# An S4D convolution and a gMLP block on one core: a planner that also hands out the cosines', parameters' and kernel products' places in PSUM, spectra of even and odd chunks kept apart, and a last chunk transformed in two halves

## The chip, the core and the metric

The kernel runs on one core of a Trainium2 chip. The core has a matrix engine (TensorE, PE in the profile; its weight loads are listed as PEld), a vector engine (VectorE, DVE), an activation engine (ScalarE, ACT), GpSimd (POOL) and SyncE (SP), which here only issues transfers. Each engine works through its own queue in order. All five meet through semaphores. The operands lie in SBUF; the matrix engine writes to PSUM, which has room for eight places of 128 x 512 float32 words. The metric is the device time of one execution in microseconds (us); lower is better.

## The reference, cut to what matters

```python
h  = x + ssm(layernorm(x))                 # x: 1 x 2048 x 512
h2 = h + gmlp(layernorm(h))

def ssm(u):                                # S4D: one long convolution for each of 512 channels
    dt = exp(log_dt);  A = -exp(log_A_real) + 1j*A_imag;  C = (C_real + 1j*C_imag)*dt
    K = 2*einsum("dn,dnl->dl", C, exp(A*dt*l)).real        # 128 terms, 2048 positions
    return irfft(rfft(u, 4096) * rfft(K, 4096))[:2048] + u*D_skip

def gmlp(x):
    z = gelu(x @ w_in);  z1, z2 = halves(z)
    g = w_sp @ layernorm(z2) + b_sp
    return (z1 * g) @ w_out
```

Everything is float32, and the large products of the gMLP are made from three float32r products each (high x high, high x low, low x high).

## The kernel before, in words

The first phase (`phase_a`) makes the convolution. The 512 channels are four **chunks** of 128. The kernel K of a chunk comes from eight **units**, 16 channels each, so there are 32 units. A unit (function `unit`) does this: TensorE makes the phases of 2 x 512 exponentials (tile `ph`, two PSUM places); ACT and DVE take off whole turns (ACT into `cs`, which is a part of `wb`; DVE into `f`); ACT takes sines into `ph` and cosines into `ce` (a PSUM place) and back into `cs` (SBUF); POOL makes three tables of magnitudes (`m`, a part of `wa`) from the chunk's tables `mt`; DVE multiplies the sines and cosines by them; TensorE forms the kernel piece with 32-wide products, back into the first half of `ph`; ACT copies it to one of six buffers `ks`. `ph` exists twice, and the second unit waits for the first one's copy to `ks` before it can write there again.

The two transforms are products too, cut into pieces. Per chunk there are eight of each: **a** (first step of the input's transform, 8 matmuls), **b** (second step, 4 matmuls; its result is the spectrum `ka`), **c** (first step for the kernel, from `ks`), **d** (second step for the kernel, 4 matmuls, whose PSUM result DVE multiplies into `ka` and `kb`), and **e** (back transform from `ka` and `kb`, 8 matmuls). Between b and d two transfers write `kb`, which is `ka` with its halves of partitions exchanged. The pieces a, b, c and e are copied out of PSUM by ACT. All pieces and all small steps take their PSUM places from three tiles `fft`. There is one pair `ka`, `kb`, so b of a chunk waits for e of the chunk before.

Ahead of the first unit stand the parameters of chunk 0 (`params`: some twenty DVE and ten ACT instructions on 128 x 128, then eight transfers to DRAM, `scr_stk`, from where POOL's queue loads `sw`, the left operand of a unit's first product), the tables `mt`, and the layer norm of the input (`norm_x`, 64 statistics on DVE, then 64 scalings that ACT, DVE and POOL share by the fixed string `NORM`). The parameters of chunk 1, and those of 2 and 3 together, come between the first units.

The order of all that is set by a planner (class `Plan`). Each call on an engine is recorded with a duration and its dependences, `list_schedule` lays them out forwards and backwards by rules of engine, PSUM place and shared SBUF port, `schedule` repeats it with random shifts and keeps the shortest plan, and the calls are then issued in the plan's order. Since `issue` makes all these calls, nearly all of phase A's instructions have one line in the profile, L424. They are told apart by tile.

Next come `phase_b1` (last step of the back transform, tile `y`, L882; layer norm; first half of the gMLP's input product, L916), `phase_b2` (second half, L965) and `phase_b3` (mixing over positions, L1051; output product, L1034). They are ordered by the framework, not by `Plan`. The transfers that `phase_b1` needs (`xq`, `g`, `w1r`) are issued by SP as soon as phase A's buffers under them are free, and the split of `w1r` (L808, L809) stands inside phase A's last pieces: it is issued behind the copy that `last` names.

Of the kernel before, what the change touches and what calls it, by code (L numbers as in the profile page):

```python
# [12 lines left out]
I32 = mybir.dt.int32  # L13
# [13 lines left out]
NORM = "aavaapav"  # L27
# [4 lines left out]
TRIES = 60  # L32
# [145 lines left out]
class Plan:  # L178
# [4 lines left out]
    HOP = 0.2  # L183

    def __init__(self, nc, banks):
        self.nc, self.banks, self.ops, self.live, self.t, self.step = nc, banks, [], {}, 0.0, 0.0
        self.nbank, self.open = 0, None
        for e in self.ENGINES:
            setattr(self, e, _Engine(self, e))
# [4 lines left out]
    def bank(self, shape):  # L194

        self.nbank += 1
        n = math.prod(shape[1:])
        names = "abc"[:len(shape) - 1]
# [4 lines left out]
    @contextmanager  # L203
    def group(self, dur):

        self.open = dict(calls=[], aps=[], eng=None, dur=dur)
        yield
        g, self.open = self.open, None
        self._add(**g)

    def _resolve(self, x, bank=None):
        return x.view(self.banks[0] if bank is None else bank) if isinstance(x, Late) else x

    def call(self, e, method, args, kw, dur=None):
# [10 lines left out]
        return self._add(calls, aps, e, dur)  # L225

    def _add(self, calls, aps, eng, dur):
        e, method, args, kw = calls[0]
        o = dict(id=len(self.ops), eng=self.ENGINES[eng], calls=calls, t=self.t, deps={}, banks=set(), func=None, lat=0.0)
        self.t += self.step  # L230
        o["port"] = False
        views = [(self._resolve(x), w) for x, w in aps]
        spaces = [str(v.space) for v, _ in views]
        out, ins = views[0][0], [v for v, w in views[1:] if math.prod(v.shape[1:]) > 1]
        n = math.prod(out.shape[1:])
        isps = ["PSUM" in str(v.space) for v in ins]
        if o["eng"] == "DVE":
            ins = ins or [out]
            two = method not in ("tensor_scalar", "tensor_scalar_add", "tensor_scalar_mul", "tensor_copy", "memset", "bn_stats",
                                 "reciprocal")  # L240
            c = math.prod(ins[0].shape[1:]) if method == "bn_stats" else n
            ps = any(isps) or "PSUM" in str(out.space)
            if two or ps or method == "bn_stats":
                d = 0.15 + c / 960
            elif method == "reciprocal":
                d = 0.15 + c / 160
            else:
                d = 0.15 + c / 1920
            o["port"] = not ps and method not in ("bn_stats", "reciprocal", "memset")
        elif o["eng"] == "ACT":  # L250
            d = 0.18 + n * 0.00083
            f = str(args[2]).split(".")[-1] if method == "activation" else "Copy"
            o["func"] = {"Exp": "exp", "Sin": "sin", "Arctan": "sin"}.get(f)
        elif o["eng"] == "POOL":
            d, o["port"] = 0.3 + n * 0.0022, True
        elif o["eng"] == "PE":
            d = 0.4
        else:
            d = 0.06
        if method == "dma_start":  # L260
            nb = 4 * out.shape[0] * n if out.shape else 0
            o["lat"] = 2.0
            o["dma"] = nb / 250e3
            o["port"] = False
            if o["eng"] == "POOL":
                d = 0.7
        o["dur"] = dur if dur is not None else d
        for (x, w), (v, _) in zip(aps, views):
            key = x.key if isinstance(x, Late) else v.tensor.name
            if isinstance(x, Late):  # L270
                o["banks"].add(x.key)
            if isinstance(key, str) and key.startswith("in_"):
                continue
            self._touch(o, key, v, w)
        o["names"] = {v.tensor.name for v, _ in views}
        self.ops.append(o)
        return o
# [27 lines left out]
    def prepare(self):  # L305
# [8 lines left out]
        for ids in holders.values():  # L314
            for i in ids[1:]:
# [9 lines left out]
    def list_schedule(self, want, back=False):  # L325
# [9 lines left out]
        ready, free = {e: [] for e in engines}, {e: 0.0 for e in engines}  # L335
        est, start, end = [0.0] * n, [0.0] * n, [0.0] * n
        banks, held, until, uses = [(0.0, i) for i in range(len(self.banks))], {}, {}, dict(self.uses)
        port = dma = last = 0.0
        table = None
        for i in range(n):  # L340
            if not left[i]:
                ready[ops[i]["eng"]].append(i)
        for _ in range(n):
            best = None
            for e in engines:
                cand = []
                for i in ready[e]:
                    t = max(est[i], free[e])
                    if i in self.bank_of and self.bank_of[i] not in held:
                        if not banks:  # L350
                            continue
                        t = max(t, min(banks)[0])
                    if ops[i]["port"]:
                        t = max(t, port)
                    cand.append((t, i))
                if cand:
                    soon = min(cand)[0] + 0.25
                    w, i, t = min((want[i], i, t) for t, i in cand if t <= soon)
                    if best is None or (t, w, i) < best:
                        best = (t, w, i)  # L360
            t, _, i = best
            o = ops[i]
            e = o["eng"]
            ready[e].remove(i)
            b = self.bank_of.get(i)
            if b is not None and b not in held:
                x = min(banks)
# [801 lines left out]
```

## Time and profile before

Three runs took 988.8, 991.05 and 990.53 us (median 990.53). The profiled execution took 990.94 us.

| | us |
|---|---|
| profiled execution | 990.94 |
| its span, first to last instruction | 989.2 |
| PE busy in the span | 866.9 |
| DVE busy | 546.4 |
| ACT busy | 397.2 |
| POOL busy | 230.1 |
| first y matmul (end of phase A) | 393.95 |

Times below are counted from the span's start. A row of a grouped view gives line, engine, operation, "out<-in", shapes, count, then the busy time in us and the mean duration of one in ns, then the engine's idle time just before these instructions and what ended it. "fft", "ka", "wb" and so on are tiles; `x` is the tile x1 (the input's first step, and before that the parameters of chunk 0), `a` is a2 (a constant). One matmul of these float32 products is two rows in counts from the trace and one in the listings of the order.

### The profile page before, as it was taken

To read this page: it belongs to the slowest core of one execution; us is meant where nothing else is said; L and a number is where in the kernel's file an instruction comes from. 1 tells how busy PE (TensorE), PEld (TensorE's weight loads), DVE (VectorE), ACT (ScalarE), POOL (GpSimd) and SP (SyncE) were. 2 spreads that over 40 slices of the span, in tenths; PEclk is the share of its full clock that TensorE was granted. 3 is DMA by queue.
4 is the path that set the end of the run, shared out by engine and by line. 5 is a ranking of instruction groups with operands and counts; after the bars stand their busy time and mean duration, and the time that the engine had idled before them with its cause. 6 is when DMAs were issued, how large, how long until landed. Compare 5 with 4: busy or idle time off the path is not lost.

```text
span 989.2 us, 16700 instructions
## 1 busy us (share of the span) xinstructions
PE 866.9 (88%) x6936; PEld 735.0 (74%) x6936; DVE 546.4 (55%) x994; ACT 397.2 (40%) x657; POOL 230.1 (23%) x185
## 2 busy tenths in 40 slices
PE   0245798988989978889999999999999999999994
PEld 0134687867978868878889998888888888888883
DVE  6989979998669743955427783135113311431142
ACT  4287868758766723153434442122012201211110
POOL 3656575668764600000001110000000000000010
PEclk9999999989999978989999999999999999999997
DMA  9102220061040194645341113124223422332221
GB/s 343 32 17 99 63 55 2 12 143 34 10 108 12 34 338 174 181 129 138 119 159 43 32 32 107 54 66 126 65 63 96 129 59 80 88 105 64 64 64 53
DMA packets 45386, 88.84 MB, mean 90 GB/s; under 512 B 4480, under 2 KB 19712, under 8 KB 42880
## 3 DMA queue, kind: packets, MB, share of 16 engines
q1 hardware_dynamic: 43872, 85.17, 28.7%
q0 software_dynamic: 1440, 2.62, 1.0%
q8 instruction: 54, 0.88, 0.4%
q14 instruction: 20, 0.16, 0.1%
HBM read 59.99 MB, written 19.40 MB: 80 GB/s over the span
## 4 chain that ended last, share of the span: by engine, by line
PE 77%; DVE 15%; ACT 3%; issue 3%; DMA 1%; SPq 0%; DVEq 0%; ACTq 0%
PE g L1051 31%; PE fft L424 14%; PE pz L916 8%; PE pz L965 8%; PE po L1034 6%; PE ph L424 5%; DVE f L424 3%; DVE ka L424 3%; PE y L882 3%; DVE wb L424 2%; DVE big L424 2%; PE pl L1034 2%; DVE kb L424 1%; DVE wa L424 1%; DVE x L424 1%
## 5 line engine op out<-in xcount | busy, mean ns | idle before, releaser
L1051 PE MATMUL g<-wts,z 128*128 128x512 f32 x1008 | 233.0, 391 | 0.0
L1051 PEld LDWEIGHTS g<-wts,z 128*128 128x128 f32 x1008 | 189.3, 188 | 41.5
L424 POOL TENSOR_TENSOR wa<-mt 128x512 f32<-128x512 f32 x96 | 153.2, 1620 | 90.8 <-DVE wb L424 49.9
L809 DVE TENSOR_TENSOR wts<-raws,wts 128x512 fp32r<-128x512 f32 x64 | 44.1, 690 | 187.9 <-ACT wts L808 187.9
L808 ACT CAST wts<-raws 128x512 fp32r<-128x512 f32 x64 | 39.7, 621 | 255.9 <-PE g L1051 251.9
L1086 POOL TENSOR_TENSOR sums<-sums,zo 128x512 f32<-128x512 f32 x3 | 4.3, 1417 | 365.2 <-DVE sums L1081 359.2
L965 PE MATMUL pz<-w,ht 128*128 128x448 f32 x384 | 77.4, 363 | 0.0
L965 PEld LDWEIGHTS pz<-w,ht 128*128 128x128 f32 x384 | 72.0, 187 | 5.3
L916 PE MATMUL pz<-ht,w1h 128*128 128x512 f32 x224 | 71.5, 398 | 0.0
L971 POOL TENSOR_SCALAR sm<-sm 128x1 f32<-128x1 f32 x16 | 3.8, 240 | 235.2 <-DVE sm L970 235.2
L424 DVE SCALAR_TENSOR_TENSOR f<-wb,ph 128x1024 f32<-128x1024 f32 x32 | 38.7, 1217 | 31.0 <-ACT wb L424 30.8
L424 ACT COPY big<-fft 128x512 f32<-128x512 f32 x64 | 36.4, 585 | 41.2 <-PE fft L424 41.2
L424 PE MATMUL fft<-c_inv,ka 128*128 128x128 f32 x256 | 52.2, 287 | 0.8 <-DVE ka L424 0.8
L1034 PE MATMUL po<-w,gz 128*128 128x512 f32 x216 | 52.2, 396 | 0.0
L424 PE MATMUL fft<-c_inv,kb 128*128 128x128 f32 x256 | 50.3, 280 | 0.0
L916 PEld LDWEIGHTS pz<-ht,w1h 128*128 128x128 f32 x224 | 42.8, 191 | 9.6
L1034 PEld LDWEIGHTS po<-w,gz 128*128 128x128 f32 x216 | 40.6, 188 | 9.5
L916 PE MATMUL pz<-ht,w1l 128*128 128x512 f32 x112 | 44.9, 401 | 0.0
L424 DVE TENSOR_TENSOR f<-ph,wa 128x512 f32<-128x512 f32 x64 | 41.9, 681 | 1.9 <-ACT ph L424 1.5
L424 PEld LDWEIGHTS fft<-c_inv,ka 128*128 128x128 f32 x256 | 39.8, 197 | 3.3 <-issue 1.6
L424 PE MATMUL ph<-f 128*32 128x64 f32 x1024 | 23.1, 236 | 20.9 <-DVE f L424 20.9
L424 PE MATMUL fft<-big,a 128*128 128x128 f32 x256 | 37.0, 301 | 5.0 <-DVE ka L424 4.2
(162 smaller groups left out, 1581.5 us busy)
## 6 DMA issues: line engine op xcount, KB each, us to landing
raws<-in_w_sp_dram SPq DMA_DIRECT2D x64, 256.0 KB, 2.7
kb<-ka SPq DMA_DIRECT2D x8, 1024.0 KB, 11.4
g<-in_c_g_dram SPq DMA_DIRECT2D x8, 1024.0 KB, 4.9
scr_z<-zo SPq DMA_DIRECT2D x28, 256.0 KB, 2.0
big<-in_u_a_dram SPq DMA_DIRECT2D x8, 512.0 KB, 9.7
xq<-in_u_b_dram SPq DMA_DIRECT2D x4, 1024.0 KB
scr_h<-xq SPq DMA_DIRECT2D x16, 256.0 KB, 3.9
sums<-scr_z SPq DMA_DIRECT2D x16, 256.0 KB
```

Source lines behind the costliest of these rows:

```text
L424: r = getattr(getattr(self.nc, e), method)(*[real(x) for x in args], **{k: real(x) for k, x in kw.items()})
L808: nc.scalar.copy(hi, src)
L809: nc.vector.tensor_sub(lo, src, hi.bitcast(F32))
L882: nc.tensor.matmul(py[:, i, :], gt[:, i, r, :], qv[:, r, l0 + i], start=(r == 0), stop=(r == 1))
L916: nc.tensor.matmul(pt, w[:, q, f], ht[n][k][:, q], start=(q == 0 and i == 0), stop=(q == 3 and i == 2))
L965: nc.tensor.matmul(pt[:, :FQ], a[:, q], w2[:, b, q, f], start=(q == 0 and i == 0), stop=(q == 3 and i == 2))
L971: nc.gpsimd.tensor_scalar_add(sm[:, 14:15], sm[:, 13:14], 1e-5)
L1034: nc.tensor.matmul(pt, gz[fb][:, x, P * a:P * a + P], wo[:, y, fb, :], start=(fb == 0 and i == 0), stop=(fb == FB - 1 and i == 2))
L1051: nc.tensor.matmul(gs[fb], z2[si][:, x, f], w[:, y], start=(si == 0 and i == 0), stop=(si == 15 and i == 2))
L1086: (nc.gpsimd if fb % 2 else nc.vector).tensor_mul(gl_[fb], gl_[fb], z1)
```

## The change

The planner now hands out all eight PSUM places: two double ones and four single ones (`WIDE = 2`). A unit's `ph` takes a double place; its two cosines take one place each, both written to PSUM; the kernel product takes a place of its own instead of the first half of `ph`. The parameters' and the layer norm's working values lie in PSUM places too. The parameters are made in two goes, chunk 0 alone and chunks 1 to 3 together (128 x 384). A call may have alternatives (`either`): a copy out of PSUM is ACT's or DVE's, a scaling in `norm_x` is ACT's or POOL's, four small steps of the parameters are DVE's or POOL's. `ka`, `kb` and `x1` become three slots `trio`: even chunks have their spectrum in slot 0, odd ones in slot 2, the exchanged one is always slot 1; x1 moves into a slot of `big`. DVE's two products of a piece d become one of twice the length. The last chunk's d and e are done in two halves of 16 channels-columns: its first half needs only the first four units' kernels. The planner's durations and its search are different (fixed `STEPS` instead of 60 random tries). The other phases' code is unchanged.

```diff
-NORM = "aavaapav"
-TRIES = 60
+STEPS = ((10001, 0.7), (10005, 0.7), (10007, 3.0), ...)
+WIDE = 2
@@ class Plan
-    HOP = 0.2
+    HOP = dict(PE=0.3, DVE=0.05, ACT=0.05, POOL=0.08, SP=0.1)
+    OVER = dict(PE=0.0, DVE=0.08, ACT=0.1, POOL=0.05, SP=0.0)
+    LIMITS = {2: 2, 3: 1}
+    def either(self, *thunks):
+        self.alts = []
+        for th in thunks:
+            th()
+        alts, self.alts = self.alts, None
+        o = self._add(**alts[0])
+        o["forms"] += [self._form(**a) for a in alts[1:]]
...
@@ phase_a
-    x1, kab = one(w1, "x1", [SLOT]), [one(w1, t, [SLOT]) for t in ("ka", "kb")]
+    trio = one(w1, "trio", [3, SLOT])
-    ph_bufs = [one(ps, f"ph{i}", [2, W]) for i in range(2)]
-    ce = one(ps, "ce", [W])
-    nc = Plan(tc.nc, [one(ps, f"fft{i}", [W]) for i in range(FFT_BUFS)])
+    nc = Plan(tc.nc, [one(ps, f"ps{i}", [2, W] if i < WIDE else [W]) for i in range(8 - WIDE)])
...
-    raw1 = load_params(pm1, 1, 1)
+    raw1 = load_params(pm1, 1, NCH - 1)
...
+            nc.either(
+                lambda: nc.scalar.activation(o, i, AF.Identity, bias=nmr[:, j:j + 1], scale=r, dur=0.58),
+                lambda: nc.gpsimd.tensor_scalar(o, i, m, r, op0=ALU.subtract, op1=ALU.mult, dur=1.08))
...
@@ unit
+        ph = nc.bank([P, 2, W], 2)
-        nc.scalar.activation(ce, cs[:, 1, :], AF.Sin, bias=half_pi, scale=-TWO_PI)
-        nc.scalar.activation(cs[:, 0, :], cs[:, 0, :], AF.Sin, bias=half_pi, scale=-TWO_PI)
+            ce, cw = nc.bank([P, 1, W], 0), nc.bank([P, W], 0)
+            nc.scalar.activation(ce, cs[:, 1:2, :], AF.Sin, bias=half_pi, scale=-TWO_PI, dur=0.70)
+            cosines = nc.scalar.activation(cw, cs[:, 0, :], AF.Sin, bias=half_pi, scale=-TWO_PI, dur=0.70)
-        kp = ph[:, 0, :256].rearrange("p (d h j) -> p d h j", d=4, h=2)
+        kp = nc.bank([P, 4, 2, 32], 0)
-        nc.vector.tensor_mul(cs[:, 0, :], cs[:, 0, :], m[:, 2, :])
+        nc.vector.tensor_mul(cs[:, 0, :], cw, m[:, 2, :])
...
+    def evac(out, src):
+        return nc.either(lambda: nc.scalar.copy(out, src, dur=0.59), lambda: nc.vector.tensor_copy(out, src, dur=0.68))
...
+    def spectra(c):
+        v = [trio[:, i].rearrange("p (d k q) -> p d k q", k=NK1, q=4) for i in range(3)]
+        return v[2 * (c % 2)], v[1], trio[:, c % 2:c % 2 + 2]
...
-    def piece_d(c, g):
-        pt = st2(x1k, g)
-        for t in ab:
-            last[1] = nc.vector.tensor_mul(of_group(t, g), by_channel(pt), of_group(t, g))
+    def piece_d(c, g, lo, n):
+        kn = P // n
+        pt = bank("s2", [P, n, kn, 4])
+        with nc.group(0.23 * kn):
+            for j in range(kn):
+                nc.tensor.matmul(pt[:, :, j, :].rearrange("p d q -> p q d"), a2v[:, kn * g + j, :], x1k[:, kn * g + j, :, lo:lo + n],
+                                 start=True, stop=True)
+        v = spectra(c)[2].rearrange("p i (d k) -> p i d k", d=32)[:, :, lo:lo + n, 4 * kn * g:4 * kn * g + 4 * kn]
+        last[1] = nc.vector.tensor_mul(v, pt.rearrange("p d k q -> p d (k q)").unsqueeze(1).to_broadcast([P, 2, n, 4 * kn]), v)
...
-        if s == 0:
+        if s == 6:
             last[0] = e
...
+            split = [(0, 32, 8.5)]
+        else:
+            split = [(0, 16, 5.5), (16, 16, 8.5)]
```

The order on the engines changes from the first row on. Three places matter below. The first is TensorE's queue at the end of phase A. Before, behind the last products of a kernel piece (`ph<-wa,wb`), with the pieces c (`fft<-wb,ks`), d (`fft<-big,a`, each row a piece of 4 matmuls or two) and the first e:

```order
L424 MATMUL fft_107<-wb,ks_87 64x128 x8
L424 MATMUL ph_103<-wa,wb 32x64 x16
L424 MATMUL fft_106<-wb,ks_84 64x128 x8
L424 MATMUL ph_104<-wa,wb 32x64 x16
L424 MATMUL fft_108<-wb,ks_85 64x128 x8
L424 MATMUL fft_107<-big,a_80 128x128 x4
L424 MATMUL fft_107<-big,a_80 128x128 x8
L424 MATMUL fft_106<-c_inv,ka 128x128
```

Now, where all places are called `ps`, a piece e is `ps<-c_inv,trio`, a piece d of a half is `ps<-big,a 128x4x16`, and `ps<-f` and `ps<-wb,ident` are the phases of the last unit:

```order
L486 MATMUL ps_104<-big,a_80 128x4x16 x8
L486 MATMUL ps_103<-big,a_80 128x4x16 x8
L486 MATMUL ps_105<-big,a_80 128x4x16 x8
L486 MATMUL ps_106<-big,a_80 128x4x16 x8
L486 MATMUL ps_104<-wb,ks_82 64x128 x8
L486 MATMUL ps_103<-f_98 32x64 x16
L486 MATMUL ps_103<-wb,ident 128x4
L486 MATMUL ps_103<-wa,wb 32x64 x16
L486 MATMUL ps_105<-c_inv,trio 128x128 x8
L486 MATMUL ps_106<-c_inv,trio 128x128 x8
L486 MATMUL ps_104<-wb,ks_83 64x128 x8
L486 MATMUL ps_103<-c_inv,trio 128x128 x8
```

Four pieces d (of the first half) now stand ahead of the last kernel product (`ps_103<-wa,wb`), and the first three pieces e behind it; behind the last row shown come four more pieces d and five more pieces e. Before, all pieces d of the last chunk and all pieces e stood behind the last kernel product.

The second place is TensorE's queue up to the eighth unit's second product, the product of `wa` and `wb` in the last row but one before and in the last row now (rows between them are left out). Before, from the sixth unit on (`x_81` is x1, so `fft<-x_81,a` is a piece b):

```order
L424 MATMUL fft_108<-x_81,a_80 128x128 x4
L424 MATMUL fft_107<-x_81,a_80 128x128 x4
L424 MATMUL fft_106<-wb,ks_84 64x128 x8
L424 MATMUL ph_103<-wa,wb 32x64 x16
L424 MATMUL fft_108<-wb,ks_89 64x128 x8
L424 MATMUL ph_104<-wa,wb 32x64 x16
L424 MATMUL fft_106<-wb,big 64x128 x8
```

Now (`ps<-wb,big` is a piece a, `ps<-big,a 128x128` a piece b):

```order
L486 MATMUL ps_103<-wb,big 64x128 x8
L486 MATMUL ps_104<-wb,big 64x128 x8
L486 MATMUL ps_106<-wa,wb 32x64 x16
L486 MATMUL ps_105<-big,a_80 128x128 x4
L486 MATMUL ps_103<-big,a_80 128x128 x4
L486 MATMUL ps_104<-wb,wa 64x128 x8
L486 MATMUL ps_105<-wa,wb 32x64 x16
```

Eight pieces a of chunk 1 (from the first row to the second), its eight pieces b (from the fourth to the fifth) and one piece a of chunk 2 (the last row but one) moved ahead of the eighth unit's second product. Before, the first piece a of chunk 1 (`fft<-wb,big`) stood behind it.

The third place is ACT's queue at the first unit, whose first instruction is `wb<-ph` (now `wb<-ps_101`). Before:

```order
L424 ACTIVATE mt_98<-mt_98 128x2304
L424 ACTIVATE big<-big,ka 128x2x64 x4
L424 ACTIVATE wb<-ph_103,wb 128x1024
L424 ACTIVATE wb<-ph_104,wb 128x1024
L424 ACTIVATE big<-big,ka 128x2x64
```

Now (`big<-big,trio` is a scaling of the layer norm, 128x384 the parameters of chunks 1 to 3):

```order
L486 CAST trio<-trio 128x3x128
L486 ACTIVATE big<-big,trio 128x2x64 x18
L486 ACTIVATE ps_105<-ps_105 128x384
L486 ACTIVATE trio<-ps_105 128x384
L486 ACTIVATE big<-big,trio 128x2x64 x3
L486 ACTIVATE big<-big,trio 128x2x64
L486 ACTIVATE wb<-ps_101,wb 128x1024
```

Scalings of the layer norm (23 instead of 4) and the activations of chunks 1 to 3's parameters moved ahead of the first unit.

More of the change, by code (lines that the diff above doesn't have):

```diff
@@ L260, in _add @@
[L260 to L268, printed above, removed]
+        ps = any("PSUM" in str(v.space) for v in ins + [out])
+        if method == "dma_start":
+            f["dma"] = 4 * out.shape[0] * n / 250e3
+            d = 0.7 if f["eng"] == "POOL" else 0.06
+        elif f["eng"] == "DVE":
+            one = ("tensor_scalar", "tensor_scalar_add", "tensor_scalar_mul", "tensor_copy", "memset")
+            if method == "reciprocal":
+                d = 0.15 + n / 160
+            elif method == "bn_stats":
+                d = 0.28
+            else:
+                d = 0.15 + n / (1920 if method in one and not ps else 960)
+                f["port"] = not ps and method != "memset"
+        elif f["eng"] == "ACT":
+            d = 0.2 + n * 0.00082 + 0.08 * any(hasattr(kw.get(k), "offset") for k in ("bias", "scale"))
+            func = str(args[2]).split(".")[-1] if method == "activation" else "Copy"
+            f["func"] = {"Exp": "exp", "Sin": "sin", "Arctan": "atan"}.get(func)
+        elif f["eng"] == "POOL":
+            d, f["port"] = 0.25 + n * 0.0025, True
+        else:
+            d = 0.4
@@ L334, in list_schedule, with places, offer @@
         engines = sorted(set(self.ENGINES.values()))
-        ready, free = {e: [] for e in engines}, {e: 0.0 for e in engines}
-        est, start, end = [0.0] * n, [0.0] * n, [0.0] * n
-        banks, held, until, uses = [(0.0, i) for i in range(len(self.banks))], {}, {}, dict(self.uses)
+        ready, free = {e: {} for e in engines}, {e: 0.0 for e in engines}
+        est, start, end, took = [0.0] * n, [0.0] * n, [0.0] * n, [None] * n
+        banks, held, until, uses = [0.0] * len(self.banks), {}, {}, dict(self.uses)
+        limits = dict(self.LIMITS)
+        size = [2 if b.shape[1] == 2 else 1 for b in self.banks]
+        never = float("inf")
         port = dma = last = 0.0
         table = None
+        def places(b):
+            k = self.kinds[b]
+            if not limits.get(k, 1):
+                return []
+            return [(t, size[i], i) for i, t in enumerate(banks) if t < never and (size[i] == 2 or k < 2) and (size[i] == 1 or k != 0)]
+        def offer(i):
+            for f in ops[i]["forms"] if forms is None else [forms[i]]:
+                ready[f["eng"]][i] = f
         for i in range(n):
             if not left[i]:
-                ready[ops[i]["eng"]].append(i)
+                offer(i)
         for _ in range(n):
@@ L419, in real @@
         def real(x):
[L420 removed]
+            return x.view(self.place(x.key, o["bank"])) if isinstance(x, Late) else x
         r = None
@@ L800, in rest @@
             done[o["id"]] = nc.issue(o)
-            if o is last[0]:
+            if o in last and all(x["id"] in done for x in last):
                 yield [done[x["id"]] for x in last]
```

382 lines of the change are left out of this document (212 added, 170 removed).

## The prediction

> **What bounds the kernel now.** I read the busy time by stretches first, because the averages of the whole span mix phase A with the gMLP. The cuts are the first unit's first DVE instruction (49.34), the eighth copy to `ks` (133.03), the break in the last kernel product (352.78) and the first y matmul (393.95). Columns: stretch, its length, busy time of PE, PEld, DVE, ACT and POOL with counts, granted clock, DMA share, GB/s.
>
> ```profile
> core 0: us, PE busy (x) PEld busy (x) DVE busy (x) ACT busy (x) POOL busy (x), PEclk, DMA share, GB/s
> 0.00:49.34 49.34, 7.89 (x21) 4.72 (x21) 39.57 (x141) 18.34 (x34) 25.61 (x25) 1.00 0.52 188
> 49.34:133.03 83.69, 52.72 (x831) 43.04 (x832) 75.23 (x109) 64.96 (x117) 48.49 (x34) 0.96 0.25 69
> 133.03:352.78 219.75, 200.47 (x3184) 173.22 (x3180) 183.26 (x233) 164.91 (x242) 138.87 (x92) 0.98 0.20 46
> 352.78:393.95 41.17, 30.71 (x220) 29.01 (x219) 14.04 (x20) 8.80 (x14) 0.00 (x0) 0.79 0.69 274
> 393.95:989.20 595.25, 575.16 (x2688) 485.02 (x2688) 234.32 (x492) 140.19 (x253) 17.13 (x35) 0.99 0.30 88
> ```
>
> There are five stages, each with its own limit. In the first DVE works 40 of 49 us. In the second, the first eight units, DVE is busy 75.23 of 83.69 (90%) and PE 63%. In the third PE is busy 200.47 of 219.75 (91%), DVE 83%. In the fourth PE waits a quarter of the time, at a clock of 0.79. The fifth is PE alone (97%), and its code and order stay. So all gain or loss lies ahead of 393.95.
>
> Then the chain of waits, in order of time, over the end of phase A:
>
> ```profile
> 348.15 1.09 PE fft L424 x16
> 351.42 1.36 PE ph L424 x55
> 352.78 5.32 issue
> 358.09 0.65 PE ph L424 x11
> 359.24 2.00 PE fft L424 x16
> 361.26 0.59 ACT big L424
> 361.90 5.48 PE fft L424 x24
> 367.83 0.69 DVE ka L424
> 373.96 2.06 PE fft L424 x8
> 376.79 16.50 PE fft L424 x128
> ```
>
> Behind the last kernel product nothing overlaps: a piece c, its copy, the d pieces and their products, and then 16.5 us of e (128 rows, eight pieces of 2.06).
>
> **The change, part by part.** The durations are those of the profiled execution, so the sum is made against its 990.94, 0.4 above the median of 990.53.
>
> *Start (49.34).* Chunk 0's parameters and the rates of POOL's tables now come earlier, but 23 scalings of the layer norm stand on ACT ahead of the first unit instead of 4, and more POOL work stands ahead of the loads of `sw`.
>
> ```profile
> 34.36 0.61 POOL L424 DMA_DIRECT2D sw<-scr_stk  x1 [1.39 <-DMA scr_stk<-x]
> 37.18 0.77 PE L424 MATMUL ph<-c_kw,sw 128*128 128x512 f32 x1 [1.15 <-DMA sw<-scr_stk]
> L424 ACT ACTIVATE wb<-ph,wb x32: 1081/1114/1121, 48.2 to 341.7; 128x1024 f32<-128x1024 f32 x32
> L424 ACT ACTIVATE big<-big,ka 128x128 f32<-128x128 f32 x36 | 17.1, 590 | 0.1
> ```
>
> The phases stood ready at 40, and ACT took them up at 48.2. These 8 to 10 us of slack cover a later `sw`; the 19 additional scalings (at 17.1/36 = 0.475 us, 9 us) fill ACT where it was busy 18.34 of 49.34. I cost the stage at nothing, with bounds of -3 (the earlier rates) and +6 (if `sw` comes 8 us later than the slack allows for on top of ACT's queue).
>
> *The first eight units (83.69).* DVE is the limit there. What stands on it beside the units' work:
>
> ```profile
> L424 DVE TENSOR_TENSOR big<-big 128x256 f32<-128x256 f32 x3 | 5.1, 1692 | 0.0
> L424 DVE TENSOR_SCALAR big<-big,ka 128x128 f32<-128x128 f32 x8 | 4.8, 618 | 0.0
> L424 DVE SCALAR_TENSOR_TENSOR kb<-kb 128x128 f32<-128x128 f32 x6 | 4.3, 718 | 0.0
> L424 DVE TENSOR_TENSOR kb<-kb 128x128 f32<-128x128 f32 x8 | 3.6, 458 | 0.0
> L424 DVE SCALAR_TENSOR_TENSOR ka<-ka 128x32 f32<-128x32 f32 x7 | 1.3, 189 | 0.2
> ```
>
> With their smaller kin these rows come to 28.5 us: the parameters of chunks 1 to 3 and the norm's scalings. The scalings leave DVE, most parameters move ahead of the first unit. DVE falls to about 50 and no longer decides. PE gets work instead: nine pieces a (1.09 each, the row at 348.15 has the same shape) and eight pieces b. A 128-wide matmul row is paced at 0.116 us:
>
> ```profile
> 329.72 4.63 PE L424 MATMUL fft<-x,a 128*128 128x128 f32 x40
> ```
>
> A b is eight such rows, 0.93. So PE's sum is 52.7 + 9.8 + 7.4 = 69.9, the largest. Below 70 the stage can't go; at 84 nothing is won. An engine that decides was busy for 90% (DVE here) to 91% (PE later); with ACT at 65 and DVE at 50 there is more room around it, so I take 93%: 75, **-9**.
>
> *The middle (219.75).* PE loses those 17.2 us and gets four pieces d of the last chunk's first half: 200.5 - 17.2 + 5.6 = 188.9. A half's piece is sixteen rows with 64 columns each; no row here has that shape. It lies between sixteen rows at half the pace (0.93) and at the whole (1.86), since each has the same 128-wide weights; I take the middle, 1.4. For DVE:
>
> ```profile
> L424 DVE TENSOR_TENSOR wb<-wb,wa x32: 676/685/5571, 55.1 to 347.0; 128x512 f32<-128x512 f32 x32
> L424 DVE TENSOR_TENSOR f<-ph,wa x64: 629/681/692, 53.9 to 350.0; 128x512 f32<-128x512 f32 x64
> L424 DVE TENSOR_TENSOR wb<-wb,wa 128x512 f32<-128x512 f32 x24 | 25.6, 1066 | 0.1
> L424 DVE TENSOR_TENSOR kb<-fft,kb 128x512 f32<-128x512 f32 x24 | 16.1, 683 | 1.3 <-PE fft L424 1.3
> L424 DVE TENSOR_TENSOR wa<-ce,wa 128x1024 f32<-128x1024 f32 x24 | 29.3, 1219 | 1.8 <-ACT ce L424 0.9
> L424 ACT COPY big<-fft 128x512 f32<-128x512 f32 x50 | 28.3, 584 | 12.6 <-PE fft L424 12.6
> ```
>
> The product `wb<-wb,wa`, all in SBUF, takes 0.685 in the median but up to 5.6 beside POOL's work; the one with an operand in PSUM never took over 0.692. With the cosines in PSUM it becomes the second kind: 24 x (1.066 - 0.682) = -9.2. The pieces d cost 48 x 0.683 = 32.8 before, and 28 of twice the length at 1.219 = 34.1 now, +1.3. Some 23 of the 27 copies that pass from ACT to DVE lie here, at 0.68 +15.6. The rest of the parameters (11.8) leaves. DVE: 183.3 - 4 = 179, ACT's 165 falls by 13. PE stays the limit. At before's 91.2%, 188.9 gives **207** (-13). Bounds: PE at 95%, 199; DVE again at its 83.4%, 215.
>
> What speaks against two of these moves is the small steps in PSUM. The nearest rows, one operand in PSUM and none:
>
> ```profile
> L424 DVE TENSOR_TENSOR ka<-ka,fft 128x64 f32<-128x64 f32 x2 | 0.4, 206 | 0.0
> L424 DVE TENSOR_TENSOR ka<-ka 128x64 f32<-128x64 f32 x2 | 0.4, 222 | 0.0
> ```
>
> 206 against 222 ns: no dearer, so these steps stand in the sum unchanged. The Trainium skill ("Perfetto Trace Analysis", Optimizing Scalar/DVE Operations) puts DVE's overhead per instruction at about 60 ns in SBUF and 125 in PSUM; by it some 45 small steps would cost 3 us more, an estimate from that page that these two rows don't bear out.
>
> *The end (41.17).* All e pieces still stand behind the last kernel product, since the last chunk's x and kernels meet only there, but half of the d pieces don't, and the first three e cover the last copy to `ks`. Path: e 16.5, one c 1.1, four half pieces d 4 x 1.4 = 5.6 (3.7 to 7.4), one product of DVE 1.2 that the next e waits for, the last copy 0.6, and some 2 for the rest of the kernel product and for hand-overs: **27** (-14). Lower bound 23 (faster d, no hand-overs); upper 33, if the stall of 5.32, which no engine's work explains, comes again.
>
> *Sum.* 49.3 + 75 + 207 + 27 = 358.3 instead of 393.95, -35.6. 990.94 - 35.6 = 955.3; I forecast **955**. The stages' own bounds give 938 to 970 when not all fall the same way.
>
> **The rivals.**
>
> *The room isn't used.* The second stage stays at 84, for ACT's chain of sines and copies or POOL, which now has 19 scalings instead of 8, sets the pace; in the third DVE stays at 83% (215). For it: ACT's 65 and DVE's 75 of 84 lie near each other, and POOL's products are long (the row is of the middle stage):
>
> ```profile
> L424 POOL TENSOR_TENSOR wa<-mt 128x512 f32<-128x512 f32 x69 | 110.8, 1631 | 61.6 <-DVE wb L424 33.5 <-PE ph L424 20.7 <-DVE f L424 3.7
> ```
>
> Against: POOL waits 61.6 us there for others. 49.3 + 84 + 215 + 27 = 375.3, -18.7: **972**.
>
> *It packs better.* Start 47, PE nearly without gaps in both stages (70, 199), end 24: 340, -54: **937**. For: the cosines' places and the copies that go to DVE free ACT just where PE waited for it. Against: no stage of phase A had its engine above 91%.
>
> *Strided output (slower).* A matmul of piece d now writes its row of 128 words with neighbouring words 16 apart (32 in a half), where it wrote whole runs before (`pt[:, j, :]`). Of a 128-column matmul with such an output the trace has no row. Pieces d are 24 x 0.93 + 8 x 1.4 = 33.5 us of PE, all on its path. The gain is eaten when they take 1 + 35.6/33.5 = 2.06 times as long; at 2.5 times, +50: **1005**. The Trainium skill ("PSUM — Partial Sum Buffer", Specifications (TRN2)) says of PSUM's 8-byte cachelines that any access that isn't contiguous slows matmuls significantly. By that page it would be this case, but it gives no factor and nothing in the run of before shows one.
>
> *Single places run out.* A unit now takes three of the four single places in turn, two for its cosines and one for the kernel product; before, none of these came from the three places of the pieces. If each of the 32 units holds PE up by 1.1 us more (a piece's length), the gain of 35.6 is gone: **990**. Against: pieces rarely waited for a place while there were three, as the waits for ACT's copies in this row show (1.8 us in all):
>
> ```profile
> L424 PE MATMUL fft<-wb,ks 128*64 128x128 f32 x411 | 28.6, 289 | 1.8 <-ACT x L424 0.8 <-ACT ks L424 0.5 <-ACT big L424 0.5
> ```
>
> **How the numbers follow.** Forecast 0.62, room not used 0.20, better packing 0.09, strided output 0.05, places 0.04. A range of 930 to 978 holds nearly the whole first case, most of the second and half of the third or more, and leaves out the last two: 0.8. What can be told from no change here is about 0.2%, 2 us: faster 0.92 (the first three, and a little of the others), same 0.02, slower 0.06 (strided output and the upper half of the places).
>
> **What would show it.** First y matmul near 358, with 595 behind it. The first unit's DVE start at 49 (45 to 56), the eighth copy to `ks` near 124, the last kernel product near 331. `wb<-ps,wa` at 0.68 with no long one. The full pieces d at 0.116 us a row, the halves' between 0.058 and 0.116. DVE about 50 us busy in the second stage, 179 in the third; PE's share at least 91% in both. Wrong: a first y later than 380, d rows above 0.2, or the stall of 5 us in more places than the end.

## The result, and the profile after

The changed kernel takes 953.60 us (median of four runs, 950.24 to 958.96) against 990.79 for the kernel before in the same comparison: a ratio of 0.963, 95% interval 0.9581 to 0.9678. The forecast was 955, in a range of 930 to 978. The profiled execution is the fastest of the four, 950.24 us with a span of 948.4.

The busy time by stretches, cut at the same events as before: the first unit's first DVE instruction (46.44), the eighth copy to `ks` (133.73), the end of the last kernel product (328.66) and the first y matmul (353.00). The columns are stretch, length, busy time of PE, PEld, DVE, ACT and POOL with counts, granted clock, DMA share, GB/s.

```profile
0.00:46.44 46.44, 8.20 (x25) 5.62 (x25) 37.06 (x145) 32.96 (x63) 33.90 (x38) 1.00 0.60 215
46.44:133.73 87.29, 63.90 (x1044) 54.46 (x1043) 70.94 (x91) 63.90 (x98) 56.78 (x45) 0.96 0.27 69
133.73:328.66 194.93, 187.28 (x3038) 162.74 (x3038) 174.61 (x205) 141.08 (x197) 133.84 (x89) 0.99 0.27 69
328.66:353.00 24.34, 22.91 (x213) 22.43 (x209) 8.41 (x8) 8.80 (x14) 0.00 (x0) 1.00 0.59 212
353.00:948.40 595.40, 575.32 (x2688) 485.06 (x2688) 234.83 (x493) 140.26 (x253) 17.08 (x35) 0.98 0.30 91
```

| stage | before | forecast | after |
|---|---|---|---|
| start, to the first unit | 49.3 | 49.3 | 46.4 |
| first eight units | 83.7 | 75 | 87.3 |
| middle | 219.7 | 207 | 194.9 |
| end of phase A | 41.2 | 27 | 24.3 |
| gMLP | 595.3 | 595.3 | 595.4 |

The sum came out 5.3 us below the forecast, but two of its terms missed by 12 us each, in opposite directions. The first eight units didn't get shorter, though TensorE does 11 us more work in them. The middle is shorter than forecast: TensorE is busy for 187.28 of 194.93 (96%).

TensorE idles for 23.4 us of the first eight units. Two of its waits, 12.8 us together, stand at their start, ahead of the third unit's phases and of its first product (start, duration, engine, line, operation, count, and in brackets the wait ahead of it):

```profile
54.02 0.76 PE L486 MATMUL ps<-c_kw,sw 128*128 128x512 f32 x1 [7.32 <-ACT ps L486]
67.70 1.08 PE L486 MATMUL ps<-f 128*32 128x64 f32 x32 [5.48 <-ACT big L486]
```

These are waits for the first units' own chain; in the last run below, where they are 8.45 and 5.88 us, the profile names DVE's `f` for both. The longest single wait, 8.49 us, comes later. Rows of DVE, then of POOL, then of ACT and TensorE:

```profile
88.45 1.21 DVE L486 SCALAR_TENSOR_TENSOR f<-wb,ps 128x1024 f32<-128x1024 f32 x1
89.69 10.58 DVE L486 TENSOR_SCALAR wb<-f 128x1024 int32<-128x1024 int32 x1
100.20 0.67 DVE L486 SCALAR_TENSOR_TENSOR f<-wa,ps 128x512 f32<-128x512 f32 x1
```

```profile
89.57 1.57 POOL L486 TENSOR_TENSOR wa<-mt 128x512 f32<-128x512 f32 x1
91.11 1.46 POOL L486 TENSOR_TENSOR mt<-rcs,wb 128x768 f32<-128x768 f32 x1
92.53 4.33 POOL L486 TENSOR_TENSOR wa<-mt 128x512 f32<-128x512 f32 x3
96.83 2.89 POOL L486 TENSOR_TENSOR mt<-rcs,wb 128x768 f32<-128x768 f32 x2
```

```profile
100.37 0.69 ACT L486 ACTIVATE ps<-wb 128x512 f32<-128x512 f32 x1 [8.62 <-DVE wb L486]
91.09 2.05 PE L486 MATMUL ps<-big,a 128*128 128x128 f32 x16
101.63 5.23 PE L486 MATMUL ps<-big,a 128*128 128x128 f32 x32 [8.49 <-ACT trio L486]
```

An instruction of DVE that takes 0.69 us at the median took 10.58. It began 0.12 us behind the first of seven instructions of POOL that follow each other without a break, and ended 0.5 us behind the last (96.83 + 2.89 = 99.72). Its operands, `f` and `wb`, lie in SBUF. ACT's next cosine waited 8.62 us for it, ACT's copies to `trio` stood behind that cosine, and TensorE waited 8.49 us for a place in PSUM that such a copy frees.

Not every meeting of this kind ends like that. In the middle the same instruction came in behind one POOL instruction, though the next followed at once; that next one then took 1.93 us, where its kind takes 1.49 on average (DVE's row, then POOL's):

```profile
195.33 1.92 DVE L486 TENSOR_SCALAR wb<-f 128x1024 int32<-128x1024 int32 x1
190.58 6.11 POOL L486 TENSOR_TENSOR wa<-mt 128x512 f32<-128x512 f32 x4
196.66 1.93 POOL L486 TENSOR_TENSOR mt<-rcs,wb 128x768 f32<-128x768 f32 x1
```

What decides between the two outcomes isn't shown by any run here.

The groups show what the change did to these waits. Before (first two rows) and after (last two):

```profile
L424 DVE TENSOR_TENSOR wb<-wb,wa 128x512 f32<-128x512 f32 x32 | 31.8, 997 | 0.1
L424 DVE TENSOR_SCALAR wb<-f 128x1024 int32<-128x1024 int32 x32 | 31.7, 1000 | 0.3
```

```profile
L486 DVE TENSOR_TENSOR wb<-ps,wa 128x512 f32<-128x512 f32 x32 | 21.8, 682 | 0.6 <-ACT ps L486 0.5
L486 DVE TENSOR_SCALAR wb<-f 128x1024 int32<-128x1024 int32 x32 | 40.2, 1268 | 0.2
```

The product with a cosine in PSUM lost its 10.0 us of waiting, and `wb<-f`, which is still in SBUF alone, took on 8.5.

The end of phase A, TensorE's rows behind the last kernel product (L992 is y):

```profile
328.64 3.84 PE L486 MATMUL ps<-c_inv,trio 128*128 128x128 f32 x32
332.41 1.09 PE L486 MATMUL ps<-wb,ks 128*64 128x128 f32 x16
333.43 2.05 PE L486 MATMUL ps<-c_inv,trio 128*128 128x128 f32 x16
335.32 7.26 PE L486 MATMUL ps<-big,a 128*128 128x64 f32 x64
342.42 9.15 PE L486 MATMUL ps<-c_inv,trio 128*128 128x128 f32 x80
353.00 11.43 PE L992 MATMUL y<-big,g 128*128 128x128 f32 x100 [1.43 <-ACT big L486]
```

Three pieces e cover the last copy to `ks`, as forecast, and TensorE hardly waits. The four half pieces d take 7.26 us for 64 rows, 0.113 a row, as long as rows of twice their columns. No stall stands in this stage. One of 3.00 us, which likewise ends with nothing that the profile names, came in the middle instead, just after SP had begun to issue the transfers to `g` (307.45):

```profile
311.26 0.65 PE L486 MATMUL ps<-f 128*32 128x64 f32 x30 [3.00 <-issue]
```

### The profile page after: what moved, and what is told of

Its sections match the earlier page's. It is cut to its first block, busy times and chain, and to the rows that moved or that the text cites. A ratio compares the mean times of both kernels' runs of the same rounds, so it can differ in the third digit from the quotient of the medians.

```text
span 948.4 us, 16818 instructions
## 1 busy us (share of the span) xinstructions
PE 857.6 (90%) x7000; PEld 730.3 (77%) x7000; DVE 525.8 (55%) x939; ACT 387.0 (41%) x623; POOL 241.6 (25%) x206
## 4 chain that ended last, share of the span: by engine, by line
PE 60%; DVE 1%; issue 0%; ACT 0%
PE g L1161 32%; PE pz L1026 8%; PE pz L1075 8%; PE po L1144 6%; PE y L992 3%; PE pl L1144 2%; DVE w1r L1015 0%; DVE w1r L1013 0%; PE lnh_pm L129 0%; DVE stats L997 0%; DVE raws L1147 0%; DVE xq L995 0%; DVE ht L919 0%; PE lnh_pv L138 0%; ACT big L486 0%
## 5 line engine op out<-in xcount | busy, mean ns | idle before, releaser
L486 POOL TENSOR_TENSOR wa<-mt 128x512 f32<-128x512 f32 x96 | 149.5, 1581 | 63.8 <-PE ps L486 23.3
L919 DVE TENSOR_TENSOR wts<-raws,wts 128x512 fp32r<-128x512 f32 x64 | 44.1, 689 | 188.9 <-ACT wts L918 188.5
L486 PE MATMUL ps<-big,a 128*128 128x128 f32 (+1 forms) x576 | 72.7, 283 | 11.1 <-ACT trio L486 8.5
L486 PEld LDWEIGHTS ps<-big,a 128*128 128x128 f32 x576 | 67.9, 195 | 15.4 <-ACT trio L486 8.7
L486 PE MATMUL ps<-c_inv,trio 128*128 128x128 f32 x512 | 62.4, 279 | 1.2 <-DVE f L486 1.1
L486 PEld LDWEIGHTS ps<-c_inv,trio 128*128 128x128 f32 x512 | 58.7, 192 | 4.2 <-DVE f L486 1.7
L486 ACT COPY big<-ps 128x512 f32<-128x512 f32 x74 | 42.8, 584 | 46.3 <-PE ps L486 45.0
L486 ACT ACTIVATE ps<-wb 128x512 f32<-128x512 f32 x64 | 42.9, 687 | 17.0 <-DVE wb L486 15.9
L486 DVE TENSOR_TENSOR trio<-ps,trio 128x1024 f32<-128x1024 f32 (+2 forms) x34 | 38.6, 1171 | 12.8 <-PE ps L486 12.7
L486 DVE SCALAR_TENSOR_TENSOR f<-wb,ps 128x1024 f32<-128x1024 f32 x32 | 38.8, 1217 | 12.2 <-ACT wb L486 12.0
```

What stands on the lines that cost most here:

```text
L486: r = getattr(getattr(self.nc, e), method)(*[real(x) for x in args], **{k: real(x) for k, x in kw.items()})
L919: nc.vector.tensor_sub(lo, src, hi.bitcast(F32))
```

## The experiments

Most of the runs keep the changed kernel's order on every engine and its places, and exchange single instructions in it (`swap` below), so that nothing else is laid out anew. Where the order had to be found again, the run with other seeds is what they are held against. Ratios are to the kernel before, with their 95% intervals.

| run | us | ratio | interval |
|---|---|---|---|
| the change | 953.6 | 0.963 | 0.9581 to 0.9678 |
| other seeds | 964.5 | 0.9745 | 0.9716 to 0.9774 |
| last chunk whole, same order | 956.8 | 0.9659 | 0.9635 to 0.9684 |
| one cosine in SBUF, same order | 955.8 | 0.9663 | 0.9648 to 0.9679 |
| all copies on ACT, same order | 955.3 | 0.9654 | 0.964 to 0.9668 |
| norm without POOL, same order | 957.8 | 0.9672 | 0.9644 to 0.9701 |
| d in whole runs, same order | 953.2 | 0.9618 | 0.9597 to 0.9639 |
| one pair of spectra, new order | 976.0 | 0.9852 | 0.9825 to 0.988 |
| four parts undone, new order | 970.7 | 0.9791 | 0.9764 to 0.9819 |
| f in PSUM, nine units, same order | 951.3 | 0.9597 | 0.9561 to 0.9633 |
| no SBUF-only instruction beside POOL's runs, same order | 945.7 | 0.9566 | 0.9543 to 0.9589 |

### Other seeds

```diff
-STEPS = ((10001, 0.7), (10005, 0.7), (10007, 3.0), ...)
+STEPS = ((1, 0.7), (2, 0.7), (3, 3.0), (4, 3.0), (5, 3.0), (6, 1.5), (7, 0.7), (8, 0.3))
```

> The changed kernel with eight other seeds of the same sizes for the search, so that all of phase A is laid out anew. Theory (the gain comes from the room that the change makes: one set of eight places, work that leaves DVE, pieces d ahead of the last product): another order finds most of it too, 950 to 965 us, first y matmul at 350 to 364. Rival (the gain is this one order, found by the search): at least 970, first y at 370 or later.

964.5 us, the first y matmul at 367.4. The time is at the upper edge of what the theory allows, and the first y is a little outside of it. This one other order finds two thirds of the gain, and the order that the change brings with it is worth 11 us more. So an experiment whose order is found again can't show an effect of a few us.

### The last chunk whole

```diff
@@ same order; swap: behind the last kernel product
-[first half's d and e at their places], 4 half pieces d, pieces e
+8 pieces d of 4 matmuls with 128 columns, one product of DVE each, then 8 pieces e
```

> The changed kernel in its own order, but the last chunk's pieces d are whole again (eight of 4 matmuls with 128 columns) and stand, with all eight e behind them, where the second half's d stood. The halves' 128 rows took as long a row as whole ones (7.26 us for 64), so they cost 7.2 us of TensorE more than whole pieces. Theory: behind the last product stand c 1.1, its copy 0.6, d 7.4, a product 1.2, e 14.8, a copy 0.6 and 0.4 for the copy to ks, 26 to 28 us against 24.3, while up to 7 us of d leave the middle stage, where TensorE is 96% busy: first y at 347 to 356, 948 to 957 us, no difference that can be told or a small gain. Rival (the halves carry the shorter end of 17 us): first y at 362 or later, 962 us or more.

956.8 us, first y at 359.9. The time lies in the theory's range and the first y between the two. Behind the last product stand 32.4 us, not the 26 to 28 expected. TensorE's rows and DVE's:

```profile
330.59 9.17 PE L486 MATMUL ps<-big,a 128*128 128x128 f32 x64 [0.69 <-ACT big L486]
342.54 14.56 PE L486 MATMUL ps<-c_inv,trio 128*128 128x128 f32 x128 [2.78 <-DVE trio L486]
359.88 10.31 PE L1027 MATMUL y<-big,g 128*128 128x128 f32 x90 [2.78 <-ACT big L486]
```

```profile
334.48 8.01 DVE L486 TENSOR_TENSOR trio<-ps,trio 128x1024 f32<-128x1024 f32 x7 [0.49 <-PE ps L486]
```

I had left out that DVE multiplies each piece for 1.22 us, more than TensorE needs for it (0.93), so DVE paces eight pieces in a row. The granted clock adds to it: it was 0.50 from 330.60 to 333.00, and TensorE's first rows there took 0.21 us each, against 0.11 at a clock of 1.00 from 335 on. And the middle hardly got shorter (the last product ended at 327.45 instead of 328.66), although 7 us of TensorE's work had left it: TensorE was busy for only 5.59 of the 9 us from 318 to 327, with waits for the units' copies and products and one of 1.82 us for which the profile names nothing. So at the end of the middle the units' own chain decides, not TensorE. The halves make phase A's end 8 us shorter here; the medians, 3 us apart, don't separate.

### One cosine back in SBUF

```diff
@@ same order and places; swap in every unit
-ACT: cw <- sin(cs[:, 0]);   DVE: cs[:, 0] <- cw * m[:, 2]
+ACT: cs[:, 0] <- sin(cs[:, 0]);   DVE: cs[:, 0] <- cs[:, 0] * m[:, 2]
```

> The changed kernel in its own order and with its own places, but one of the two cosines is written back to SBUF as before, so that its product has no operand in PSUM. Theory: the product's mean goes from 0.68 to about 1.0 us with single ones of 3 us and more, DVE +10 us in all, most of it beside TensorE's work in the middle stage: 953 to 962 us. Rival (the PSUM operand carries the gain of the middle stage): 965 or more. If it is hidden altogether: 952 to 955.

955.8 us. The product was held up again (982 ns on average), but no single one took more than 2.02 us, and `wb<-f` keeps the longest wait (min/median/max in ns):

```profile
L486 DVE TENSOR_TENSOR wb<-wb,wa x32: 678/796/2015, 52.9 to 327.1; 128x512 f32<-128x512 f32 x32
L486 DVE TENSOR_SCALAR wb<-f x32: 679/689/10383, 50.2 to 322.0; 128x1024 int32<-128x1024 int32 x32
```

The rival is out: a PSUM operand in this one product doesn't carry the middle's gain.

### All copies on ACT

```diff
@@ same order and places; swap
-27 copies out of PSUM on DVE
+27 copies out of PSUM on ACT
```

> The changed kernel in its own order and with its own places, but the 27 copies out of PSUM that DVE makes are made by ACT, at 0.585 us, 16 us more on ACT and 18 less on DVE. Theory: ACT was 73% busy in both the second and the third stage and has the room, but single copies come late behind sines: 955 to 963 us. Rival (sharing the copies carries the gain): 968 or more; rival (it does nothing): 951 to 955.

955.3 us, at the lower edge of the theory. The longest `wb<-f` became 5.9 us, and TensorE's waits for ACT's copies to `big` rose from 6.9 to 12.9 us in sum. By itself the sharing of copies isn't the gain.

### One pair of spectra, and four parts undone

Two first runs of these had an error of mine: the pieces b of a chunk were issued ahead of d and e of the chunk before and overwrote its spectrum, so they compute something else, and nothing is read from them.

> The changed kernel's planner, its eight common places and its new parameters stay, and four things are undone together: all copies out of PSUM on ACT, one of the two cosines in SBUF, one pair of spectra for all chunks, the last chunk whole. All of phase A is laid out anew, so the kernel with other seeds (964.5) is what it is held against. Theory (the pieces of the change are worth something together, though copies and cosine singly cost 2 us each): 972 to 988 us. Rival (planner and places carry nearly all): 968 or less. Rival (they carry nothing): 988 or more.

> The changed kernel with one pair of spectra for all chunks: the pieces b of a chunk wait for the pieces e of the chunk before, as they did before the change. Laid out anew, so it is held against the kernel with other seeds (964.5). Theory (the pieces a and b of a later chunk filled TensorE, and can't any more): 968 to 980 us. Rival (order by itself finds other work): 958 to 967.

Repeated in the right order:

```diff
-        return v[2 * (c % 2)], v[1], trio[:, c % 2:c % 2 + 2]
+        return v[0], v[1], trio[:, 0:2]
@@ pieces b of chunk c + 1 behind e of chunk c; x1u in the third slot of trio
@@ four undone: also every copy on ACT, one cosine in SBUF, last chunk whole
```

> As the run with four things undone (all copies out of PSUM on ACT, one of the two cosines in SBUF, one pair of spectra, the last chunk whole; new planner, common places, new parameters), but now the pieces b of a chunk are issued behind the pieces e of the chunk before, and the input's first step has the third slot to itself, as before the change. In the earlier run and in the earlier run with one pair, b overwrote the spectrum ahead of d and e, so they computed something else and their times say nothing. Held against the kernel with other seeds (964.5). Theory: 970 to 986 us. Rival (planner and places carry nearly all): 968 or less. Rival (they carry nothing): 988 or more.

> The changed kernel with one pair of spectra alone, issued in the right order and with the input's first step in the third slot. Held against the kernel with other seeds (964.5). Theory (a and b of later chunks can't fill TensorE any more): 968 to 980 us. Rival (order by itself finds other work): 958 to 967.

970.7 and 976.0 us: both as the theory said. With all four parts undone 20 of the 37 us are still there; the planner, the eight common places, the parameters in two goes and the norm's sharing bring them together, and no run here parts these. The single pair costs 11.5 us against the run with other seeds. Both orders were found anew, and two orders of one kernel can lie 11 us apart, so the time alone wouldn't say much; TensorE's rows do:

```profile
327.23 1.10 PE L486 MATMUL ps<-wa,wb 128*32 128x64 f32 x64
335.00 1.87 PE L486 MATMUL ps<-wb,ks 128*64 128x128 f32 x14 [4.44 <-issue]
336.79 20.74 PE L486 MATMUL ps<-big,a 128*128 128x64 f32 x96
357.33 7.77 PE L486 MATMUL ps<-c_inv,trio 128*128 128x128 f32 x48
```

The last kernel product ended at 328.33, as early as in the changed kernel (328.66), but 50.7 us stood behind it, with all pieces d (96 + 32 half rows) among them: the first half's d can't stand ahead of the last product while the chunk before still holds the only pair. The halves need the second slot. What this order costs by itself isn't shown by the 50.7, though. A wait of 4.44 us for which the profile names nothing lies in it, and behind it the granted clock (last but two in this row) fell to 0.50 and stayed there until 357.5:

```profile
337.00:347.00 10.00, 10.00 (x48) 10.00 (x49) 2.45 (x2) 0.48 (x1) 0.00 (x0) 0.50 1.02 415
```

The 96 half rows took 0.216 us each instead of the 0.113 of the changed kernel, an estimated 10 us more. Whether the single pair brings the wait and the low clock with it stays open; the kernel before had both at its end too (5.32 us, and 0.50 from 358.09 to 362.00). That the run with four parts undone is faster than the one with one part undone would fit halves that only cost with a single pair, but its clock differed as well (0.72 at its pieces d).

### The norm without POOL

```diff
@@ same order and places; swap
-19 scalings of the layer norm on POOL
+19 scalings of the layer norm on ACT
```

> The changed kernel in its own order and places, but the 19 scalings of the layer norm that POOL makes are made by ACT (0.45 us each, 8.6 us more there, 16 us less on POOL). Theory (POOL's stretches of work hold DVE up): the longest |f| shrinks from 10.6 us to 8 or less, but the first unit starts up to 4 us later behind ACT's longer queue: 950 to 956 us. Rival (POOL's scalings were a gain of the change): 958 or more. If the hold-up goes with them entirely: 949 or less.

957.8 us, between theory and rival. The first unit started 1.6 us later, but the long instruction stayed:

```profile
95.35 10.54 DVE L486 TENSOR_SCALAR wb<-f 128x1024 int32<-128x1024 int32 x1
```

My reading of it fell: the seven POOL instructions beside it in the changed kernel's rows above are the units' products and the tables (`wa<-mt`, `mt<-rcs`), none is a scaling.

### d in whole runs

```diff
@@ same order and places; swap in every piece d
-PE: pt[:, d, j, q] (words 16 or 32 apart)      DVE: reads runs
+PE: pt[:, j, q, d] (neighbouring words)        DVE: reads by steps
```

> The changed kernel in its own order and places, but every piece d writes PSUM in whole runs (neighbouring words next to each other), and DVE's product reads them by steps instead. Tells what paces a half's rows at 0.113 us. Theory (the 128-wide weights do, not the columns): 64 rows of the second half stay at 7.2 to 7.3 us, 950 to 956 us. Rival (the stride of 32 words does): 64 rows in 3.7 to 4.5 us, the end 3 us shorter, 948 to 951. Whole pieces at 0.11 to 0.12 us a row in both cases. If DVE is slowed by its steps, its product grows over 1.22 us.

953.2 us. The half rows take what they took. Whole pieces (in one group with the pieces b, 285 ns before the swap) and DVE's product (1218 ns) don't differ either:

```profile
337.30 7.26 PE L486 MATMUL ps<-big,a 128*128 128x64 f32 x64
```

```profile
L486 PE MATMUL ps<-big,a 128*128 128x128 f32 x448 | 58.4, 286 | 12.1 <-ACT trio L486 8.5 <-DVE trio L486 2.5 <-ACT ks L486 1.0
L486 DVE TENSOR_TENSOR trio<-ps,trio 128x1024 f32<-128x1024 f32 x32 | 37.7, 1217 | 12.8 <-PE ps L486 12.8
```

The stride costs nothing here. What stays the same between whole and half pieces is the 128-wide weights; that they set the pace is argued from this, no run changes them. The Trainium skill ("TensorE: Matmul & The Clock Gate", LDWEIGHTS (loading the stationary operand)) gives a weight load's time as its columns divided by 1.2, in ns: 107 for 128, whatever the matmul's own columns. The 0.113 us a row agrees, for 64 columns as for 128; the profile's own records of single loads are longer (195 ns on average in `ps<-big,a`) and overlap. The sentence on slow strided access that the prediction cited from its PSUM page finds no support in these rows of float32.

### What holds the first eight units up

```diff
@@ same order and places; swap in units 0 to 8
-DVE: f <- (cs - MAGIC) - ph;    DVE: cs <- |f|;    ACT: ph <- sin(f)
+DVE: ph <- (cs - MAGIC) - ph;   DVE: cs <- |ph|;   ACT: ph <- sin(ph)
```

As the sine now overwrites what |ph| reads, |ph| is issued ahead of it; on DVE it moved forward past a few other instructions, and the rest of the order stays.

> The changed kernel in its own order and places, but in the first nine units the phases without whole turns (f) are written in place in PSUM, so that DVE's next instruction, which makes |f|, has an operand there and isn't held up beside POOL's work (one took 10.58 us from 89.7 on, TensorE waited 8.5 us behind it). It then takes 1.22 instead of 0.69 us. Theory (that one hold-up sets the second stage): eighth copy to ks 6 to 9 us earlier, 944 to 949 us. Rival (POOL's own products come late for the unit anyway, and take over the wait): 950 to 956.

951.3 us, the eighth copy to `ks` at 132.9: no DVE instruction of the nine units took over 1.23 us, and nearly nothing was won. The rival, in its number. But its reason isn't the one I gave. The next instructions of DVE that lie in SBUF alone were held up instead (DVE's row, POOL's, TensorE's):

```profile
72.12 8.28 DVE L487 TENSOR_SCALAR trio<-trio,wb 128x128 f32<-128x128 f32 x3
```

```profile
71.16 8.77 POOL L487 TENSOR_TENSOR wa<-mt 128x512 f32<-128x512 f32 x6
```

```profile
80.06 1.08 PE L487 MATMUL ps<-ident,trio 128*128 128x128 f32 x3 [6.63 <-DVE trio L487]
```

The last run takes these three away too:

```diff
@@ besides: same order and places; swap in the parameters
-DVE: mx <- co * dts * 2;   DVE: rcs <- transposed (PSUM)
+ACT: mx <- co * dts;       DVE: rcs <- 2 * transposed (PSUM)
```

> The run with f in PSUM for nine units, and also the parameters' three scalings that held DVE up there (8.28 us from 72.1 on for three instructions of 0.3 us, all in SBUF, while POOL worked without a break from 71.2 to 79.9; TensorE waited 6.6 us for their transposes) are made by ACT, which waited for 6 us there; the factor 2 goes into DVE's copy from PSUM behind the transposes. Order and places are those of the changed kernel. Theory (the hold-up moves to DVE's next instruction that lies in SBUF alone; with it gone too, TensorE gets the time): no DVE instruction over 3 us between 50 and 133, eighth copy to ks at 124 to 129, 941 to 948 us. Rival (units and POOL's products pace these eight units by themselves): eighth copy at 130 or later, 949 to 953.

945.7 us (five runs, 944.49 to 948.44), ratio 0.9566. No DVE instruction between 50 and 133 was held up, and TensorE's wait of 6.6 us is gone. The seventh and the eighth copy, in the changed kernel (first row) and now (second), and now's first y (third):

```profile
133.03 0.70 ACT L486 COPY ks<-ps 128x256 f32<-128x256 f32 x2
128.57 0.63 ACT L487 COPY ks<-ps 128x256 f32<-128x256 f32 x2
348.95 7.30 PE L1009 MATMUL y<-big,g 128*128 128x128 f32 x63 [1.43 <-ACT big L487]
```

The eighth copy ends 4.5 us earlier, and the first y comes 4.1 us earlier. The time is in the theory's range, the eighth copy (129.2) just behind it. By the medians this kernel is 7.9 us (0.8%) faster than the change; the two intervals still touch between 0.9581 and 0.9589, and the two profiled executions, of which the change's is its fastest, lie 4.6 us apart. It is the fastest of all kernels here.

The Trainium skill ("SBUF — State Buffer", Who interferes with whom) says that DVE and GpSimd share a pair of ports which the one that begins first holds for the whole instruction while the other is fully blocked, and that a DVE instruction with at most one SBUF input, outside the fast modes, doesn't take part. The rows agree as to who is blocked. They add that the wait isn't always over after one instruction of POOL: in the row at 89.69 it lasted for seven, in the one at 195.33 for one.

## Why the prediction was right, point by point

**The start (0, bounds -3 and +6): right in kind.** It came out at -2.9, the lower bound. ACT was busy 32.96 of 46.44 us with the additional scalings, and took the phases up at 45.3 instead of 48.2.

**The first eight units (75): wrong, the largest miss.** The step that failed is "DVE falls to about 50 and no longer decides". DVE was busy 70.94. DVE's groups of this stage that make most of the difference:

```profile
L486 DVE TENSOR_SCALAR wb<-f 128x1024 int32<-128x1024 int32 x9 | 17.4, 1946 | 0.1
L486 DVE COPY big<-ps 128x512 f32<-128x512 f32 x12 | 7.9, 686 | 6.3 <-PE ps L486 6.0 <-ACT wb L486 0.3
L486 DVE COPY trio<-ps 128x512 f32<-128x512 f32 x3 | 2.1, 692 | 0.8 <-PE ps L486 0.8
```

Of the 20 us above the forecast, 10 are these 15 copies: I had put 23 of the 27 in the middle. Some 6 more are `wb<-f`, 17.4 us for nine instead of 11.4 for nine before, which I took over in the sum without asking which instruction POOL's work would hold up next. The 93% share for TensorE was chosen from engines that had reached 90 and 91%; it reached 73%. Of the 23.4 us that TensorE idled, 8.5 are the wait behind the DVE instruction of 10.58 us, and 12.8 the two waits for the first units at the start. With the hold-ups gone, in the last run, the stage still took 82.4 us (46.78 to 129.20), with TensorE at 78% and DVE busy for 63.56: they account for 4.9 of the 12 us by which the stage missed, and the rest is mostly the start of the units' chain, which the sum had left out and no run here changes. TensorE's own work was over-estimated too, 69.9 for 63.90. A unit's first product takes 1.08 us at 67.70 and 0.65 from 84.20 on, where the kernel before still took 1.08 at 83.63; the granted clock is 1.00 in both stretches, so the reason stays open. The first rival ("the room isn't used", 84) is what this stage did, in part for its reason (the units' chain) and in part for one that it didn't name.

**The middle (207): too long.** TensorE's work was forecast at 188.9 and measured 187.28. The step that failed is the share, "at before's 91.2%": it was 96%, as the second rival (199) had it. DVE, forecast at 179, measured 174.61. The term -9.2 for the cosine's product held (10.0 over the whole phase); what it didn't foresee is that the wait moves to `wb<-f`, most of it in the stage before.

**The end (27, from 23 to 33): right, with one term mis-sized.** 24.34. The half piece d, taken as 1.4, took 1.81 and lies near its upper bound of 1.86. That it came out lower all the same is due to other terms: the five last e took 9.15 us (1.83 each) at a clock of 1.00, not 2.06 at 0.79, and of the 3.8 us for a product of DVE, a last copy and hand-overs only the 1.43 ahead of y is left. The stall went to the middle, as 3.00 us.

**The gMLP (no change): right.** 595.40 after 595.25.

**The rivals.** Strided output: out, by the run with whole runs. Single places run out: not in every unit, as that rival had it. TensorE's longest wait, 8.49 us, was for a place, but for one that ACT's copy held behind the long DVE instruction. Room not used and better packing: each true of one stage, and they cancel to within 0.2 us. That the sum of 955 came so near to the result is luck in this respect; two of its four parts were wrong by 12 us.

**What the gain consists of.** No part that could be exchanged within the order cost more than 4.2 us by itself (956.8, 955.8, 955.3 and 957.8 against 953.6), and these steps are within the spread of the change's own runs. The larger blocks are the 20 us that stay with four parts undone and the 11 us of the order; as the orders were found anew, these can't be added up exactly. What the planner alone would do with the old places stays open.

## What to carry to other kernels

When an instruction is freed from a contention, ask which is the next of its engine that is exposed to the same: here two cures only moved the wait, and the third one paid. Cost a stage by its worst single wait on the chain, not by a share of busy time taken over from another stage. And compare parts of a searched schedule inside one frozen order, with one run of another order to show how large the search's own part is.

## What the runs showed of the hardware

A DVE instruction with all its operands in SBUF can be kept out by POOL instructions that follow each other at once: one waited 10 us for seven of them, three others took 8 us beside six. It isn't always so; at 195.33 one came in behind the first, in 1.92 us. DVE's instructions of the units with an operand in PSUM took 0.68 us for 512 columns and 1.22 for 1024 all along. A float32 matmul row with 128-wide weights takes 0.11 us with 64 columns as with 128, in whole runs or with words 32 apart, at a granted clock of 1.00; at 0.50 it took 0.21 us with 128 columns and 0.216 with 64. The prediction had the 64 columns' time as its upper bound, and long waits only for the product with a cosine.
